# Turning q and k in four quadrants of TensorE beside the score steps, with score steps that run over pair borders

## The chip, the cores and the metric

The kernel runs on one core of one Trainium2 chip. The time is the device time of one launch in microseconds, the median of several runs. A profile of one execution (its trace) shows what each engine did: PE is TensorE's matrix products and PEld its weight loads, DVE is VectorE, ACT ScalarE, POOL GpSimd, SP the engine that mostly issues DMAs.

## What is computed

Attention with a threshold over 8 batches of 8 heads, 576 rows and a head size of 64, all in float32, and then a mixer (a low rank product over the rows and a two-layer channel network) on the result:

```python
scores = scale * np.matmul(q, k.transpose(0, 1, 3, 2))
thresh = np.max(scores, axis=-1, keepdims=True) - tau
scores = np.where(scores >= thresh, scores, -1000000000.0)
attn = np.exp(scores - np.max(scores, axis=-1, keepdims=True))
attn = attn / (np.sum(attn, axis=-1, keepdims=True) + 1e-09)
x = np.matmul(attn, v)                # heads side by side: [8, 576, 512]
h = x.transpose(0, 2, 1) @ U @ V      # rank 32, over the rows
u = x + h.transpose(0, 2, 1)
out = u + np.maximum(u @ w_ch1, 0.0) @ w_ch2      # 512 -> 2048 -> 512
```

## The kernel before

**Tiling.** Two heads of one batch make a pair, 32 pairs in all, worked in couples (two pairs, 64 and 64 columns of the model each). The 576 rows of a head are nine sets of 64 (every ninth row); a full tile is two sets, 128 rows, so a pair has four full tiles and a half one (tile 4), and the half tiles of the two pairs of a couple are put together into one step. A couple is thus nine score steps: tiles 0 to 4 of the first pair and 0 to 3 of the second. There are 144 steps, each with two heads.

**Loads and turning.** `load_tasks` brings q and k of a pair into `qkraw` (rows on the partitions, nine slots of 2 x 64 numbers; slot 4 holds q's tile 4 in the lower partitions and k's in the upper) by eight DMAs, on POOL's queue for all pairs but the first. Scores need the head's 64 numbers on the partitions, so `prepare_tasks` turns them: `turn_main` makes four TensorE transposes of 128x128 for q (L518) and four for k, each four into one PSUM bank, and `copy_main` (L524, ScalarE) copies the bank to `qkT`; `turn_rest` makes one transpose for the two half tiles (L531), `copy_rest` (L537) copies it. `qkT` is a ring of two, `qkraw` too. A pair's loads wait until the turns of the pair two before are done.

**Scores.** `scores` (L587) makes one or two steps in one task. Each product takes 64 partitions (one head) and gives 64 rows, so TensorE runs as four quadrants of 64x64: the row half is the head, the column half the half of the tile. The moving k is cut into two pieces (`PIECES`). PSUM has eight banks of 512 float32 columns; six of them are two `trio` tiles, one for each head, and two steps side by side (slots 0 and 1) fill the columns 224 to 1376 of a trio (`score_cols`). A task of two steps therefore holds all six banks, one of a single step holds banks 0, 1, 3 and 4 (`KEPT`). All other products (transposes included) use the array as 128x128.

**Softmax.** For each step and head, `weigh` (L616, VectorE) scales the scores into a buffer `s_sb` (a ring of seven) and takes their minimum after the sign is turned; `threshold` (L632) and `exponential` (L639) run on ScalarE; `select` (L646, VectorE) compares, multiplies and sums into `w_ring`. POOL copies the last columns twice (L664), a DMA transpose on SP's queue (or TensorE, L677) turns the weights, and `product` (L746 to L754) multiplies them with v. Then come the low rank products (L811, L826), the sums into x, and for each batch `mixer_tasks`: `up` (L930), `rest` (L946) and `down` (L963), whose outputs leave through the ring `o` of three. Where TensorE would be idle at the start, `fill` issues products without use (L421).

**Order.** Nothing is ordered by hand line by line: `Order.run` is a planner that runs when the kernel is built. Each piece of work is a `Task` with an engine, an estimated cost, the tasks it depends on and the banks it takes. The planner walks through time, at each step starts the task that can start first on some engine, with the ready time plus a table of offsets (`OFF`, by kind of task and stage) as its order, and so writes a fixed order for each engine. It gives PSUM banks (`KEPT` for score tasks, any free bank for others), counts a cost for changing TensorE between quadrants and the whole array (`SWITCH`, `PARTS`), and takes mixer products by due times counted in score steps (`DUE`). `BankOrder` declares which accesses of the two trios need an order, bank by bank.

The loop at the end makes nine steps for a couple: up to pair 1 all alone, from then on the first alone and the other eight by twos.

Of the kernel before, what the change touches and what calls it, by code (L numbers as in the profile page):

```python
# [68 lines left out]
P = 128  # L69
# [7 lines left out]
DM = H * D  # L77
# [10 lines left out]
LONE = 2  # L88

# [4 lines left out]
DUE = (461, 86.25, 1468.5, 516.25, 1049.25, 748, 134.75, 1357.5)  # L94
# [33 lines left out]
class Order:  # L128
# [8 lines left out]
    BEFORE = 0.45  # L137
    PATIENCE = (0, 0.2, 0.1, 0.9, 1.35)
# [7 lines left out]
    PARTS = {"S": "quadrants"}  # L146

    HOLD = (61.76, 61.61, 6.12, 44, 94.32, 94.08, 76.76, 0.01, 9.57)
# [4 lines left out]
        "copy_main": (25.53, 63.74, -194.99, 34.77, -69.14, 17.14, -324, 37.67, -35.45),  # L153
        "copy_rest": (6.5, -40.06, -14.53, 24.12, -4.13, -20.91, -46.23, 54.32, -95.65),
        "copy_tt": (-16.03, -64.1, 20.85, -110.66, 55.87, 62.18, -42.53, -53.37, -25.08),
        "copy_u": (89.47, -53.33, 162.09, -74.19, 7.13, 9.51, -102.11, -20.31, -73.82),
        "copy_u4": (-5.3, -56.82, -16.18, -6.54, 49.93, -37.52, 64.79, -22.2, -18.99),
        "copy_w": (75.7, -4.79, -22.58, 20.52, -4.75, 68.84, -1.46, 27.15, 10.06),
        "down": (52.39, 32.35, 33.69, 38.82, 7.25, -27.49, 1.69, 19.34, 131.97),
        "exponential": (61.02, 15.66, 97.71, -26.58, 23.56, 95.43, 116.8, 90.08, 11.21),  # L160
        "finish": (-53.17, -45.71, 51.42, 30.79, -14.22, -26.29, 28.78, 16.33, -75.01),
        "first": (-56.79, 75.89, 0.92, -55.7, 35.86, -3.48, 9.68, 53.63, 1.2),
        "high": (-129.72, -35.78, 31.87, -6.58, 48.08, -20.33, -28.95, -46.46, 84.01),
        "inverse": (46.71, -32.89, 54.08, 22.1, 122.91, 38.13, 143.23, 39.39, -23.27),
        "join": (2.19, 36.38, 69.81, -65.72, -28.72, -7.68, -26.75, 24.75, -3.5),
        "load": (14.89, -38.6, -1.87, -55.09, 439, 169.52, 202.43, 266.17, -64.61),
        "low": (23.82, 3.88, -45.02, 6.6, -28.12, -60.17, -87.19, -43.1, 26.46),
        "low4": (64.5, 130.96, 545.14, -26.82, 13.94, -59.21, 35.95, 265.72, -23.85),
        "low_part": (30.38, 13.98, -26.01, -41.71, 130.31, 109.34, -20.82, -133.07, -1.88),
        "low_rank": (-57.69, 16.1, -2.98, 31.4, -60.74, 41.37, 38.61, 8.08, -35.05),  # L170
        "make": (-18.31, -192.85, -81.78, -52.29, 6.69, -18.25, 12.16, -35.09, 27.21),
        "narrow": (5.95, 39.32, -9.64, -6.72, 1.46, 29.45, -10.31, 45.69, -47.12),
        "narrow_u": (-45.99, -94.08, -136.7, -16.38, -46.01, -113.33, 15.29, 42.82, -0.02),
        "narrow_u4": (2.02, -41.08, 15.16, 12.95, 69.79, 35.67, -44.1, -54.14, 56.42),
        "norm": (60.22, 26.73, 14.75, 16.35, 28.89, -20.28, -16.45, 55.02, 19.4),
        "product": (-38.14, -97.33, -17.17, 18.14, -78.98, 56.88, 40.12, 68.18, -110.66),
        "relu": (44.72, -2.34, -31.3, -83.46, 20.06, -116.77, 10.32, 4.5, -36.91),
        "rest": (64.49, 74.43, 34.29, 18.04, -20.78, -41.41, -55.22, -17.62, 44.45),
        "scores": (-2.16, -56.15, 42.01, -69.96, -15.23, -44.76, 4.79, -16.69, -3.93),
        "select": (-41.99, 29.22, -2.51, 135.03, 570.07, 400.28, 184.53, 231.57, 188.34),  # L180
        "send": (43.87, 17.75, 5.67, -19.7, -14.51, -9.84, 285.3, 70.92, -48.56),
        "send_u": (54.83, -57.33, -16.36, 177.37, 12.48, 121.89, 19.74, 60.45, 25.84),
        "spread": (-216.88, 63.66, -12.54, -9.53, -23.32, -1.29, -122.3, 43.34, 63.38),
        "spread4": (12.62, -19.59, -18, 54.22, -34.85, 61.33, -24.98, -50.63, -66.91),
        "spread_v": (-113.69, -64.83, 6.03, 44.27, 73.51, -47.79, -27.38, 65.24, 2.79),
        "sum_u": (-64.77, 3.32, 13.18, 117.53, -78.44, -9.21, 87.33, 127.21, -64.36),
        "sum_u4": (-96.51, 65.77, 2.32, 38.3, 44.64, 21.12, -125.78, 37.98, 23.47),
        "sums": (195.64, 23.57, 47.14, -31.56, 10.32, -16.1, 35.4, 4.49, -58.98),
        "threshold": (-37.94, -91.24, -43.1, -296.86, 94.89, 36.19, 66.3, 1.07, 12.5),
        "turn4": (-36.19, -43.45, 5.14, 7.01, 54.44, -61.28, 52.57, 29.57, -92.54),  # L190
        "turn_main": (0.34, 20.57, 26.79, -161.06, 126.25, -30.36, -38.23, -14.86, -5.97),
        "turn_pe": (-0.48, -21.65, -184.33, 36.36, -95.83, 51.55, 181.65, 20.16, -43.63),
        "turn_rest": (-5.99, -37.64, -0.75, 52.43, -6.2, -61.13, -8.69, -94.49, -32.06),
        "turn_u": (-85.8, -3, -69.47, -45.79, 74.76, -7.02, 3.37, 12.83, 72.77),
        "turn_w": (45.6, -1.19, -137.3, 47.86, -48.09, 10.25, -28.07, -30.73, 72.41),
        "twin": (32.78, -132.71, -13.72, -15.07, -38.22, -14.87, -64, 49.79, 55.76),
        "up": (13.07, 75.42, -49.49, -57.58, 68.34, -48.43, 10.3, 58.82, 35),
        "values": (-37.57, -25.94, -48.38, 20.3, -54.04, 26.74, 72.56, -4.07, -32.49),
        "weigh": (-145.66, -20.29, -57.18, 79.45, -16.94, 55.31, 45.2, 33.27, 31.94),
        "weights": (-56.28, 79.24, -10.97, 18.21, -35.76, 31.57, -73.46, 67.52, 113.68),  # L200
# [13 lines left out]
    def run(self):  # L214
# [8 lines left out]
        last = [0.0] * self.nbanks  # L223
        kind = None
# [15 lines left out]
        while left:  # L240
# [5 lines left out]
            soonest = min(last[n] for n in pool)  # L246
            for e in range(5):
                cands = []
                for t in ready[e]:
                    s = max(at[e], t.ready)  # L250
                    if t.banks:
                        s = max(s, soonest)
                    if t.trios:
                        s = max([s] + [last[n] - self.BEFORE * (t.steps == 1)
                                       for n in self.KEPT[t.trios]])
                    if e == POOL and t.dma:
                        s = max(s, lanes[t.ndma - 1 - self.LANES])
                    if s < NEVER:
                        cands.append((s, t))
# [6 lines left out]
            assert best, "no task can start"  # L266
            s, t = best
# [14 lines left out]
            if t.trios:  # L282
                t.got = list(self.KEPT[t.trios])
            elif t.banks:
                t.got = [min((n for n in pool if last[n] <= max(s, soonest)),
                             key=lambda n: (n < 6, n % 3 < 2, last[n]))]
            for n in t.got:
                last[n] = NEVER
# [16 lines left out]
            for f in t.frees:  # L305
                f, part = f if isinstance(f, tuple) else (f, slice(0, 8))
                for n in f.got[part]:
                    last[n] = t.end + self.SIGNAL[e] + self.TO_PE
# [13 lines left out]
def kernel(  # L322
# [64 lines left out]
    qkraw_ring = ring("qkraw", 2, [P, 9, 2, D], FP32)  # L387
    qkT_ring = ring("qkT", 2, [P, 2, S], FP32)
    vh_ring = ring("vh", 2, [P, NT, 2, 2, D])
    NS, NE = 7, 4  # L390
# [9 lines left out]
    uT4_ring = ring("uT4", 2, [P, 4, P])  # L400
    ub_ring = ring("ub", 2, [P, 4, P])
    o_ring = ring("o", 3, [P, DM], FP32)
# [7 lines left out]
    PIECES = (((0, HC), (HC, S)), ((0, 224), (224, S)))  # L410
# [24 lines left out]
    class Batch:  # L435
# [3 lines left out]
        def __init__(self, b, before):  # L439
# [5 lines left out]
            self.tt, self.uT, self.uT4 = tt_ring[b % 2], uT_ring[b % 2], uT4_ring[b // 2 % 2]  # L445

    def load_tasks(p, pr):
# [3 lines left out]
        freed = [got("q", p - 2), got("k", p - 2), got("qk4", p - 2)]  # L451
# [21 lines left out]
        for j in range(2):  # L473
            loads["k"].append(one("k", ek, lo, slice(5, 9), slice(0, 4), j, freed))
            loads["k"].append(one("k", e3 if j else ek, hi, slice(4, 9), slice(4, 9), j, freed))
# [9 lines left out]
    class Pair:  # L485


        def __init__(self, b, hp, bt):
# [6 lines left out]
            self.qkraw, self.tT, self.vh = qkraw_ring[p % 2], qkT_ring[p % 2], vh_ring[p % 2]  # L495
# [14 lines left out]
    def prepare_tasks(p):  # L510
# [3 lines left out]
        before = [got("S", p - 2, 3), got("S", p - 2, 4)]  # L514
        for x, (name, t0) in enumerate((("q", 0), ("k", 5))):
            def turn_main(t, t0=t0):
                for i in range(4):
                    nc.tensor.transpose(bank[t.got[0]][:, i * P:(i + 1) * P],  # L518
                                        pr.qkraw[:, t0 + i, :, :], ident)

            task = add(PE, 0.44, turn_main, loads[name] + before, banks=1, kind="qk")

            def copy_main(_, x=x, task=task):
                nc.scalar.copy(out=pr.tT[:, x, 0:512], in_=bank[task.got[0]])  # L524

            done[name, p] = task
            done[name + "T", p] = add(SCA, 0.47, copy_main, [task, got(name + "T", p - 1)],
                                      frees=[task])

        def turn_rest(t):  # L530
# [568 lines left out]
```

## Time and profile before

| | |
|---|---|
| median of 13 runs | 605.24 us (601.44 to 609.05) |
| the profiled execution | 603.74 us |
| its span, first to last instruction | 602.0 us |
| busy DVE: 288 `select` of 0.860, 288 `weigh` of 0.750 us | 239.3 and 203.2 us |
| busy ACT: 288 `exponential` of 0.775 us | 217.8 us |
| the copies of q and k on ACT: 64 of 128x512, 32 of 128x128 | 37.1 and 8.5 us |
| mean granted TensorE clock | 0.996 |

The span is divided among the lines that ended last (the chain of waits); the chain can be followed from 371.7 us on and consists of TensorE's rows for the greater part:

```profile
PE 29%; DVE 4%; ACT 4%; issue 1%; DVEq 0%; ACTq 0%
```

A line of the page's fifth part reads: source line, engine, operation, output from inputs, shapes, count, then busy us and mean ns of one, then idle time of the engine just before these instructions and what ended most of it. TensorE's instructions overlap one another, so the length of one record says less than the distance between starts.

### The profile page before, as it was taken

What the parts mean: (1) busy time and instruction counts of PE and PEld (TensorE: products, weight loads), DVE (VectorE), ACT (ScalarE), POOL (GpSimd) and SP (SyncE); (2) the same over time, 40 slices, a digit from 0 to 9 for tenths busy, and PEclk for the clock granted to TensorE, in tenths of its full rate; (3) what the DMA queues carried; (4) which work ended last, traced back from release to release, by engine and by line L of the source; (5) the groups of instructions that cost most, each with busy time, mean ns of one, the idle gap of its engine ahead of it and who ended that gap; (6) DMA issues with size and microseconds to landing.
All of it is one profiled execution on the core that took longest, in us unless ns stands there. A gap on an engine that the chain in (4) does not pass through costs nothing. (4 is left out here: it accounts for less than half of the span.)

```text
span 602.0 us, 17115 instructions
## 1 busy us (share of the span) xinstructions
PE 584.3 (97%) x6249; PEld 349.6 (58%) x6249; DVE 522.3 (87%) x1399; ACT 458.3 (76%) x959; POOL 370.5 (62%) x596
## 2 busy tenths in 40 slices
PE   7998889999999999999999999999999999999996
PEld 3455665666666566555665656565566666556642
DVE  4889899999999999999988999999999999994101
ACT  5657799998799866897789865897699986784540
POOL 9968576687888864576676665776677633342000
PEclk9999899999999999999999999999999999999999
DMA  7799979987999789989999999887999987667203
GB/s 161 115 176 156 166 129 157 152 150 131 203 179 182 129 182 192 182 146 146 203 152 162 147 178 191 157 161 152 197 164 152 180 153 149 123 96 131 45 1 87
DMA packets 222771, 90.48 MB, mean 150 GB/s; under 512 B 200800, under 2 KB 213040, under 8 KB 222688
## 3 DMA queue, kind: packets, MB, share of 16 engines
q1 hardware_dynamic: 207680, 66.30, 67.2%
q0 software_dynamic: 14048, 22.76, 20.4%
q8 instruction: 49, 0.80, 0.6%
q10 hardware_dynamic: 960, 0.34, 0.2%
q14 instruction: 34, 0.28, 0.2%
HBM read 37.90 MB, written 9.44 MB: 79 GB/s over the span
## 5 line engine op out<-in xcount | busy, mean ns | idle before, releaser
L639 ACT ACTIVATE e_sb<-s_sb,m 128x576 bf16<-128x576 f32 x288 | 217.8, 775 | 42.3 <-DVE s_sb L616 32.6
L646 DVE SCALAR_TENSOR_TENSOR w_ring<-s_sb,thr,e_sb 128x576 bf16<-128x576 f32 x288 | 239.3, 860 | 8.6 <-ACT e_sb L639 3.9
L616 DVE TENSOR_SCALAR_CACHE_REDUCE s_sb<-trio 128x576 f32<-128x576 f32 x288 | 203.2, 750 | 16.1 <-PE trio L587 14.7
L587 PE MATMUL trio<-qkT 64*64 64x288 f32 (+2 forms) x2304 | 163.3, 412 | 0.5 <-DVE x L791 0.3
L664 POOL COPY w_ring<-w_ring 128x128 bf16<-128x128 bf16 (+1 forms) x168 | 71.6, 437 | 106.0 <-DVE w_ring L646 85.7
L587 PEld LDWEIGHTS trio<-qkT 64*64 64x64 f32 x2304 | 83.4, 133 | 57.0 <-issue 11.7
L458 POOL DMA_DIRECT2D qkraw<-in_q_dram x125 | 82.3, 663 | 25.0 <-PE bank L518 21.7
L798 POOL TENSOR_TENSOR x<-x,rec 128x256 f32<-128x256 f32 (+1 forms) x84 | 69.1, 825 | 37.0 <-DVE x L791 28.8
L963 PE MATMUL bank<-W2b,R 128*128 128x512 bf16 x368 | 90.1, 379 | 0.4 <-ACT qkT L524 0.3
L963 PEld LDWEIGHTS <-R 128*128 128x128 bf16 x576 | 53.8, 98 | 54.1 <-issue 1.5
L458 POOL DMA_DIRECT2D qkraw<-in_k_dram x125 | 81.3, 657 | 3.1 <-issue 2.2
L930 PE MATMUL bank<-uT,W1b 128*128 128x512 bf16 x320 | 77.8, 379 | 0.7 <-ACT R L920 0.4
L930 PEld LDWEIGHTS <-W1b 128*128 128x128 bf16 x512 | 47.1, 98 | 53.3 <-issue 5.4
L553 POOL TENSOR_TENSOR vh<-vraw_ring,vh 64x128 bf16<-64x128 f32 x64 | 55.8, 872 | 14.0 <-ACT vh L546 7.6
L750 PEld LDWEIGHTS <-wT_ring 128*128 128x128 bf16 x896 | 56.0, 98 | 7.5 <-issue 2.0
L920 ACT ACTIVATE R<-bank 128x512 bf16<-128x512 f32 x91 | 52.5, 595 | 4.8 <-PE bank L930 3.0
L930 PE MATMUL trio<-uT,W1b 128*128 128x512 bf16 x192 | 48.1, 379 | 0.2 <-DVE s_sb L616 0.2
L963 PE MATMUL trio<-W2b,R 128*128 128x512 bf16 x208 | 47.5, 379 | 0.0
L632 ACT ACTIVATE thr<-m,tau_t 128x2 f32<-128x2 f32 x144 | 42.0, 294 | 3.6 <-DVE s_sb L616 3.3
L750 PE MATMUL bank<-vh,wT_ring 128*128 128x128 bf16 x624 | 44.5, 219 | 0.0
L975 DVE TENSOR_TENSOR o<-bank,x 128x512 f32<-128x512 f32 x23 | 15.8, 688 | 32.1 <-PE bank L963 31.9
L746 PE MATMUL bank<-vh,wT_ring 128*128 128x64 bf16 x176 | 33.9, 193 | 0.0
(105 smaller groups left out, 720.1 us busy)
## 6 DMA issues: line engine op xcount, KB each, us to landing
out_dram<-o SPq DMA_DIRECT2D x71, 128.0 KB, 2.9
vraw_ring<-in_v_dram SPq DMA_DIRECT2D x32, 160.0 KB, 3.9
qkraw<-in_k_dram POOLq DMA_DIRECT2D x63, 80.0 KB, 4.5
qkraw<-in_q_dram POOLq DMA_DIRECT2D x62, 80.0 KB, 4.3
vraw_ring<-in_v_dram SPq DMA_DIRECT2D x32, 128.0 KB, 4.1
qkraw<-in_q_dram POOLq DMA_DIRECT2D x63, 64.0 KB, 3.9
qkraw<-in_k_dram POOLq DMA_DIRECT2D x62, 64.0 KB, 4.3
W1b<-in_moe_w_ch_dram POOLq DMA_DIRECT2D x8, 256.0 KB, 5.4
```

What stands on the lines that cost most here:

```text
L458: queue.dma_start(pr.qkraw[part, to, j, :], src[:, j, of, :])
L553: nc.gpsimd.tensor_tensor(out=pr.vh[part, tiles_, :, h, :], in0=raw[part, tiles_], in1=pr.vh[part, tiles_, :, 0, :], op=ALU.subtract)
L587: mm = nc.tensor.matmul(cols[part, lo:hi], a.tT[hs, 0, rows], a.tT[hs, 1, lo:hi], start=True, stop=True)
L616: nc.vector.tensor_scalar(out=s_sb, in0=score_cols(slot, x), scalar1=-scale, scalar2=None, op0=ALU.mult, op1=ALU.min, accum_out=m[:, x:x + 1])
L639: nc.scalar.activation(out=e_sb, in_=s_sb, func=ACT.Exp, bias=m[:, x:x + 1], scale=-1.0)
L646: nc.vector.scalar_tensor_tensor(out=w_sb[:, 0:S], in0=s_sb, scalar=thr_[:, x:x + 1], in1=e_sb, op0=ALU.is_le, op1=ALU.mult, accum_out=pr. ...
L664: nc.gpsimd.tensor_copy(out=w_sb[:, xs, S:640], in_=w_sb[:, xs, 512:S])
L750: nc.tensor.matmul(av[:, 2 * a + j, :], w, pr.vh[:, kt, j, :, :], start=kt == 0, stop=False)
L798: nc.gpsimd.tensor_tensor(out=x, in0=x, in1=over_sum(part), op=ALU.mult)
L920: nc.scalar.activation(out=R2[:, fts, lo:hi], in_=bank[t.got[0]].rearrange("p (f c) -> p f c", c=hi - lo), func=ACT.Relu)
L930: nc.tensor.matmul(bank[t.got[0]], W1b[:, dt, ft * P:(ft + 1) * P], bt.uT[:, dt, :], start=(dt == 0), stop=(dt == 3))
L963: nc.tensor.matmul(ch, R2[:, ft, lo:lo + P], W2b[:, ft, :], start=(ft == 0), stop=(ft == 15))
```

## The change

- q and k are no longer turned by transposes of 128x128. Each block of 64 rows and 64 numbers is multiplied with a 64x64 corner of the identity, in one of the four quadrants: 18 products for q and 18 for k of a pair. The upper 64 partitions' blocks go to one bank, the lower 64 partitions' to another, so a turn needs two banks. `turn_rest` goes away; `qkraw` has ten slots, so that q and k have a tile 4 of their own.
- Each turn is followed by two copies on ScalarE, 320 and 256 columns, out of the two banks.
- The scores of two steps move to the columns 384 to 1536 of a trio, with pieces of 128, 448, 64 and 512 columns. Columns 0 to 383 of banks 0 and 3 are left free, and the planner puts a turn into them: when a task of two steps is about to start and a turn is ready within 0.2 us, the turn is issued just before it (`forced`). A turn that comes after work in 128x128 mode without such a task is held up by 20 us in the planner's list (`LATER`), but not those of the first three pairs. A bank can now be held by two tasks (`held`, `late`).
- From the couple of pairs 4 and 5 on, steps are taken by twos over the border: the ninth step of a couple is left and goes with the first of the next.
- Rings: `qkT` three in place of two, `s_sb` six in place of seven, `o` two in place of three, one `uT4` in place of two.
- `OFF`, `DUE`, `HOLD` have other numbers; the weigh pass of slot 0 is counted to start 0.75 us ahead of the task's end in place of 0.5.

```diff
-                for i in range(4):
-                    nc.tensor.transpose(bank[t.got[0]][:, i * P:(i + 1) * P],
-                                        pr.qkraw[:, t0 + i, :, :], ident)
-            task = add(PE, 0.44, turn_main, loads[name] + before, banks=1, kind="qk")
+                for i in range(NT):
+                    for h in range(2 if i < 4 else 1):
+                        rows = slice(HB * h, HB * h + HB)
+                        for j in range(2):
+                            nc.tensor.matmul(
+                                bank[t.got[h]][D * j:D * j + D, i * HB:i * HB + HB],
+                                pr.qkraw[rows, t0 + i, j, :], ident[rows, rows],
+                                start=True, stop=True)
+            task = add(PE, 0.28, turn_main, loads[name] + before, banks=2, kind="qk" if p > 2 else "qk0")
...
             def copy_main(_, x=x, task=task):
-                nc.scalar.copy(out=pr.tT[:, x, 0:512], in_=bank[task.got[0]])
+                nc.scalar.copy(
+                    out=pr.tT[:, x, :].rearrange("p (i r) -> p i r", r=HB)[:, 0:9:2, :],
+                    in_=bank[task.got[0]][:, 0:NT * HB].rearrange("p (i r) -> p i r", i=NT))
+            def copy_rest(_, cols=cols, task=task):
+                nc.scalar.copy(out=cols[:, :, 1, :],
+                               in_=bank[task.got[1]][:, 0:4 * HB].rearrange("p (i r) -> p i r", i=4))
...
-        def turn_rest(t):
-            nc.tensor.transpose(bank[t.got[0]][:, 0:P], pr.qkraw[:, 4, :, :], ident)
...
-    PIECES = (((0, HC), (HC, S)), ((0, 224), (224, S)))
+    PIECES = (((0, 128), (128, S)), ((0, 64), (64, S)))
-        return trio[j][:, 224 + slot * S:224 + (slot + 1) * S]
+        return trio[j][:, 384 + slot * S:384 + (slot + 1) * S]
...
+            if forced:
+                t, forced = forced, None
+            elif t.trios:
+                for a in ready[PE]:
+                    if a.banks == 2 and a.ready <= s + self.BESIDE:
+                        s, t, forced = max(s, a.ready, last[0], last[3]), a, t
+                        break
...
     for p in range(0, NP, 2):
         prepare_tasks(p)
+        nine = [(p, i) for i in range(NT)] + [(p + 1, i) for i in range(4)]
+        if left:
+            score_tasks(*left, nine.pop(0))
+            value_tasks(p - 1)
         prepare_tasks(p + 1)
-        while n < 9:
-            two = p >= LONE and n
-            score_tasks(*nine[n:n + (2 if two else 1)])
-            n += 2 if two else 1
+        while len(nine) > (1 if p > LONE else 0):
+            two = p >= LONE and len(nine) < 9 or p > LONE
+            score_tasks(*[nine.pop(0) for _ in range(2 if two else 1)])
+        left = nine
```

## The prediction

> **What bounds the kernel now.** I read the engine rows of the page first, then the stages, then the order of work on TensorE in one stretch, then the rows of single groups and the waits.
>
> ```profile
> PE 584.3 (97%) x6249; PEld 349.6 (58%) x6249; DVE 522.3 (87%) x1399; ACT 458.3 (76%) x959; POOL 370.5 (62%) x596
> ```
>
> TensorE is occupied for 97% of the span, VectorE for 87%. The stages (start and end, length, then busy time and count for PE, PEld, DVE, ACT, POOL) say where each has room:
>
> ```profile
> 30.00:100.00 70.00, 63.02 (x907) 41.10 (x905) 64.21 (x181) 56.63 (x114) 46.84 (x82) 0.98 1.07 159
> 100.00:200.00 100.00, 99.06 (x1142) 63.05 (x1141) 95.88 (x258) 90.20 (x193) 79.35 (x129) 1.00 1.02 160
> 400.00:500.00 100.00, 99.69 (x1103) 60.62 (x1105) 98.27 (x264) 83.72 (x178) 63.85 (x99) 1.00 0.93 162
> 500.00:540.00 40.00, 39.68 (x391) 22.50 (x384) 39.65 (x104) 30.11 (x64) 13.63 (x21) 1.00 0.73 127
> 540.00:602.00 62.00, 57.29 (x391) 30.58 (x389) 14.81 (x31) 22.99 (x45) 5.00 (x9) 0.99 0.34 65
> ```
>
> From 100 on TensorE has almost no hole, and after 540, where VectorE has run out of softmax, TensorE still has 57 us of mixer products. So whatever is taken from or given to TensorE moves the end by as much, so long as VectorE keeps pace; from 400 to 540 VectorE is busy 137.9 of 140 us and has nothing to give. The clock is granted at 1.00 nearly throughout, so it changes no duration here.
>
> The timeline of TensorE (start, length, line, tile mode and shape, count; the distance from one start to the next is the price):
>
> ```profile
> 301.69 0.19 PE L746 MATMUL bank<-vh,wT_ring 128*128 128x64 bf16 x1
> 301.82 2.17 PE L587 MATMUL trio<-qkT 64*64 64x288 f32 x32
> 303.92 0.33 PE L531 MATMUL bank<-ident,qkraw 128*128 128x128 f32 x1
> 304.08 0.60 PE L518 MATMUL bank<-ident,qkraw 128*128 128x128 f32 x4
> 304.52 0.60 PE L518 MATMUL trio<-ident,qkraw 128*128 128x128 f32 x4
> 304.96 0.39 PE L750 MATMUL bank<-vh,wT 128*128 128x128 bf16 x4
> ...
> 307.85 1.20 PE L587 MATMUL trio<-qkT 64*64 64x288 f32 x16
> 308.98 1.90 PE L930 MATMUL bank<-uT,W1b 128*128 128x512 bf16 x8
> ```
>
> A transpose costs 0.44/4 = 0.11 us. A task of two score steps takes 303.92 - 301.82 = 2.10, one of a single step 308.98 - 307.85 = 1.13. The difference, 0.97, is 16 instructions that run four at a time, one in each quadrant: four rounds of 288 columns on average, 0.243 each, 0.84 ns per column.
>
> ```profile
> L639 ACT ACTIVATE e_sb<-s_sb,m 128x576 bf16<-128x576 f32 x288 | 217.8, 775 | 42.3 <-DVE s_sb L616 32.6
> ...
> L587 PE MATMUL trio<-qkT 64*64 64x288 f32 (+2 forms) x2304 | 163.3, 412 | 0.5 <-DVE x L791 0.3
> ...
> L587 PEld LDWEIGHTS trio<-qkT 64*64 64x64 f32 x2304 | 83.4, 133 | 57.0 <-issue 11.7
> ```
>
> ```profile
> L518 PE MATMUL bank<-ident,qkraw 128*128 128x128 f32 x140 | 21.1, 275 | 0.0
> L518 PE MATMUL trio<-ident,qkraw 128*128 128x128 f32 x116 | 18.0, 278 | 1.6 <-DVE s_sb L616 1.3
> ```
>
> The costliest groups (count, busy us and mean ns, then idle time before them) hold the row that decides. A score step has 8 products in the code (two pieces, two heads, two halves), 144 steps make 1152, and the row counts 2304: a float32 product is **two** instructions, each with its weight load. L518 has 140 + 116 = 256 = 8 x 32: a transpose is **one**.
>
> **Turning q and k on TensorE.** Taken away: nine transposes a pair, 9 x 0.109 = 0.98 us. Added: two turns of 18 float32 products of 64 columns. The upper row half gets five products in each of its two quadrants (tiles 0 to 4), the lower half four, so the longer quadrant runs 5 products = 10 passes. A pass is 64 x 0.84 = 0.054; a turn 0.54, a pair 1.08. That is +0.10 a pair, **+3.2 us** over 32 pairs. A pass of this width has no row, so I bound it. Below: one pass per product, 0.27 a turn (first rival). Above: the weight load, 133 ns by its row, shows. L518's loads last 141 and come every 109, so at least 32 of a load overlap the next; 101 x 10 = 1.01 a turn, +33 us. I take 0.054, by L587: the same load, there hidden under its pass.
>
> The Trainium skill, TensorEngine Tiling (Array Packing), section Gotcha 2: Feature Incompatibilities, speaks against the change: column tiling excludes the transpose mode for fp32 input, so that the turns must be ordinary products; the trace has float32 transposes in 128*128 mode alone. Its FP8 and Floating Point Precision, section TensorE Precision Notes, gives true fp32 four passes; the trace shows two instructions, and at four of 0.054 a turn would be an estimated 1.08 and the sum 38 us instead of 3.2. The row decides.
>
> **Fewer score tasks.** Up to pair 3 nothing changes in number (9 single tasks, then 1 + 4). The other 14 couples of pairs have 1 + 4 tasks now, 70; run over the borders they are 126 steps in 63 tasks. Seven fewer. A task costs beyond its passes 0.10 going in (301.82 against the end of L746's slot, 301.72), 0.16 within (2.10 - 8 x 0.243) and 0.05 after (L531 takes 0.16, not 0.11): 0.31, so **-2.2 us**. The pieces change from 288, 288, 224, 352 to 128, 448, 64, 512 columns: the same sum, nothing.
>
> **Turns that find no score task beside them** change the mode twice, 0.31. 58 turns from pair 3 on want one of 63 double tasks. Between none and 58 (18 us) I take one in ten, 6: **+1.9**. The first pairs' turns stand where TensorE runs fillers (L421, 84 of them), at nothing.
>
> **Copies on ScalarE.** 2 x 0.58 (128x512) + 0.27 become 2 x (0.42 + 0.37), from 128x256 at 0.367 and 0.8 ns a column more: +0.15 a pair, 4.8 us, under ScalarE's 144 us of idle time. Uncovered it would be 4.8.
>
> **The new neighbours in banks 0 and 3.** ScalarE's copies and VectorE's first weigh passes (L616) now read the same banks; I count the one as waiting for the other. No such pair exists before, so bounds: nothing, or both copies in VectorE's way, 0.79 x 58 = 46 us. After a turn the copies can start when the score task's first two rounds are through (2 x 0.107 = 0.21) and end at 0.63 and 1.00; the weigh can start after slot 0 and slot 1's first piece, 0.97 + 0.11 = 1.08. So a prompt ScalarE is in time. It is busy some 80% there; behind an exponential of 0.775 with a remainder r the weigh waits r - 0.45, on average 0.07 x 0.8 = 0.056, x 58 = 3.2 us. Only where VectorE has no room (400 to 540, a quarter) does it reach the end: **+0.8**. Behind the weigh on VectorE stand the selects, then the weight transposes on SP's queue; and the next score task waits for all four weighs.
>
> The Trainium skill, PSUM — Partial Sum Buffer, section PSUM bank collisions raise a hardware error, says that two engines on one bank and quadrant at once raise an error, two readers too, so they must be kept apart; no run here shows it yet. Without it this term is 0.
>
> **Rings.** Six score buffers, not seven: a double task fills four, so two older ones may be open, not three, and VectorE must have done more selects first, each of which waits for ScalarE. Between nothing and an exponential a task (0.775 x 63 = 49): selects wait for ScalarE 3.9 us in all today; as much again, a quarter of it felt, **+1.0**. Two output buffers are covered by a row of 16 products (3.45 us) against two issues and a landing of 2.9. Loads: eight a pair on POOL's queue as before, one tile of k moved between them. They wait for two turns of the pair two back instead of three, and the turns may now be held up to 20 us in the list:
>
> ```profile
> L458 POOL DMA_DIRECT2D qkraw<-in_q_dram x125 | 82.3, 663 | 25.0 <-PE bank L518 21.7
> ```
>
> POOL already stands 21.7 us for the turns; behind it wait the copies of the weight rows (L664). Its 38% idle and the third qkT buffer cover that; nothing counted.
>
> **Sum:** 3.2 - 2.2 + 1.9 + 0.8 + 1.0 = +4.7. The profiled span is 602.0, its execution 603.74; 606.7 and 608.4 after. The median, 605.24, is 1.5 above that execution: **610**, own range 604 to 616.
>
> **Rivals.**
> - *One pass a product* (17%). For it: no row shows a float32 product with an identity. Against: all of L587's products double, whatever their width. Turns 0.54 a pair, -14.1, with the other terms -12.6: 592.6.
> - *TensorE's holes close* (15%): the turns take no spare bank any more, so mixer products find one. TensorE idles 9.5 us between 30 and 540, 7.0 of it before 100; half to all of it back gives 605 to 600.5. Against: after 100 only 2.5 us can be had.
> - *VectorE sets the end* (15%), slower: L616 waits for copies that stand behind two ScalarE instructions. VectorE idles 24.7 us from 10 to 540, 0.43 for each of 58 turns; from there each wait counts in full. At 0.7: +15.7, 625.6. For it: 98% and 99% busy in the late stages.
> - *Turns stand alone* (6%): 40 of 58 instead of 6, +10.5, 620.5. *Weight loads show* (4%): 640.
>
> The sum as worked out keeps 43%. About 0.3%, 1.8 us, is what a measurement of this kernel can tell from no change. Of the 43, 4 fall within it and 39 are slower; of the holes' 15, 7 faster, 5 same, 3 slower; the one-pass 17 are faster but for 1; the rest, 25, slower. Faster 0.23, same 0.10, slower 0.67. The range goes from the one-pass case, 591, to the VectorE case, 626; outside lie the weight loads and the edges.
>
> **What would show it.** A turn's row in 64*64 mode with x2304 in all (two passes) or x1152 (one); the start-to-start of 36 instructions near 0.54 or 0.27. L587 still x2304, in 77 runs. Waits of L616 for the copies near 3 us or over 25. TensorE busy in 100 to 540 again above 99%, and its tail after VectorE's last select longer by some 5 us. Wrong it is if turns come in at 0.27, or if most have a 128-mode neighbour on both sides.

## The result and the profile after

The changed kernel takes 614.20 us (median of 11 runs, 610.69 to 620.42) against 605.70 of the kernel before (48 runs): a ratio of 1.0149, 95% interval 1.0122 to 1.0177. It is slower by 1.5%, about twice what was forecast (610). The profiled execution took 612.19 us, its span is 610.4 (before 602.0).

The engine rows of the page after (busy us, share of the span, count):

```profile
PE 591.4 (97%) x8295; PEld 343.5 (56%) x8295; DVE 518.8 (85%) x1399; ACT 465.0 (76%) x991; POOL 357.2 (59%) x596
```

The shares are those of before to within three points. Nothing in them tells a reader that 8 us were lost, or where. The groups of instructions answer the question of the passes, and the copies and waits:

```profile
L546 PE MATMUL trio<-ident,qkraw 64*64 64x64 f32 x1656 | 36.8, 223 | 0.6 <-DVE x L799 0.3 <-ACT wT_ring L711 0.2
L546 PE MATMUL bank<-ident,qkraw 64*64 64x64 f32 x648 | 13.9, 219 | 0.0
L611 PE MATMUL trio<-qkT 64*64 64x128 f32 (+3 forms) x2304 | 162.6, 411 | 0.2 <-DVE s_sb L640 0.2
L640 DVE TENSOR_SCALAR_CACHE_REDUCE s_sb<-trio 128x576 f32<-128x576 f32 x288 | 206.0, 750 | 27.5 <-PE trio L611 16.6 <-ACT qkT L555 5.2 <-ACT qkT L560 0.9
L555 ACT COPY qkT<-trio 128x320 f32<-128x320 f32 x46 | 19.7, 429 | 4.6 <-DVE s_sb L640 3.5 <-PE trio L611 0.8
L560 ACT COPY qkT<-trio 128x256 f32<-128x256 f32 x46 | 17.2, 374 | 7.0 <-PE trio L611 6.4
```

The turns' rows have 1656 + 648 = 2304 instructions for 1152 products: two each. The weigh passes (L640) wait 6.1 us in all for copies of q and k, a wait that did not exist before. In the timeline of TensorE a turn and its score task look like this:

```profile
307.38 1.03 PE L987 MATMUL bank<-W2b,R 128*128 128x512 bf16 x4
308.34 0.74 PE L546 MATMUL trio<-ident,qkraw 64*64 64x64 f32 x34
308.86 0.33 PE L611 MATMUL trio<-qkT 64*64 64x128 f32 x2
308.91 0.23 PE L546 MATMUL trio<-ident,qkraw 64*64 64x64 f32 x2
```

The 34 instructions take 308.86 - 308.34 = 0.52 from start to start, and the score's first two start before the turn's last two. Such a task of turn and two steps takes 2.68 in all, one of two steps alone 2.11: a turn costs 0.57. Summed over the whole trace by the distance between starts, the turns take 40.0 us of TensorE (transposes before: 36.5), the score products 152.7 (before 157.6), fillers 29.2 (114 of them; before 21.6, 84), and TensorE is idle for 10.4 (8.5).

All slots without the fillers come to 562.8 us, before to 563.9: the useful work on TensorE became **smaller** by 1.1, and the fillers and the idle time grew by 7.6 and 1.9. Fillers are issued where the planner expects TensorE to wait. The stages show where the time went. TensorE has more holes than before (99.06) between 100 and 200 us:

```profile
100.00:200.00 100.00, 98.23 (x1516) 60.11 (x1514) 91.98 (x251) 88.84 (x191) 73.94 (x122) 1.00 0.98 153
```

VectorE's rows in three stretches (start and end, length, busy time and count, clock, DMA), first before:

```profile
10.00:160.00 150.00, 139.56 (x383) 0.99 1.00 150
160.00:400.00 240.00, 227.84 (x610) 1.00 0.97 171
400.00:550.00 150.00, 144.35 (x384) 1.00 0.87 151
```

and after:

```profile
10.00:160.00 150.00, 131.21 (x364) 0.99 1.01 152
160.00:400.00 240.00, 228.18 (x613) 1.00 1.02 167
400.00:550.00 150.00, 141.79 (x384) 1.00 0.88 147
```

From 10 to 160 us VectorE did 19 instructions and 8.4 us less. From then on it kept pace in instructions (610 and 613, 384 and 384). The same can be read from the 288 selects in the timeline of VectorE (us from the span's start; this table is used throughout):

| kernel | end of select 81 | from there to select 288 | from there to the end | span |
|---|---|---|---|---|
| before | 158.4 | 387.2 | 56.4 | 602.0 |
| after | 167.8 | 387.2 | 55.4 | 610.4 |
| bf16_all | 169.0 | 383.6 | 55.4 | 608.0 |
| both_less | 166.3 | 380.8 | 56.2 | 603.3 |
| double | 184.6 | 414.2 | 55.5 | 654.3 |
| short_turns | 168.7 | 379.5 | 55.4 | 603.6 |
| short_before | 160.3 | 383.7 | 56.3 | 600.3 |
| other_list | 157.6 | 396.9 | 59.0 | 613.5 |

By select 81 (of tile and head, some nine pairs in) the changed kernel is 9.4 us late, as much as at select 288. Over the 207 selects after it both kernels take 387.2 us. The distance isn't steady, though: it is 3.6 us at select 63, 9.2 at 90, 5.3 at 120, 7.8 at 180 and 11.4 at 270 (3.2 to 12.9 in all after select 81), since the order of the selects among VectorE's other work differs too. And each row is one execution: the seven traces with the changed list and no more work than it has (after, bf16_all, bf16_early, both_less, vec_less, short_copies, short_turns) end select 81 between 166.3 and 172.5. So differences of a few us in this table tell nothing by themselves. The question for the experiments was therefore what the turns' work costs, and what the order costs that the planner wrote for everything else.

### The profile page after: what moved, and what is told of

It reads as the page before. It is cut to its first block, busy times and chain, and to the rows that moved or that the text cites. A ratio compares the mean times of both kernels' runs of the same rounds, so it can differ in the third digit from the quotient of the medians.

```text
span 610.4 us, 21337 instructions
## 1 busy us (share of the span) xinstructions
PE 591.4 (97%) x8295; PEld 343.5 (56%) x8295; DVE 518.8 (85%) x1399; ACT 465.0 (76%) x991; POOL 357.2 (59%) x596
## 5 line engine op out<-in xcount | busy, mean ns | idle before, releaser
L670 DVE SCALAR_TENSOR_TENSOR w_ring<-s_sb,thr,e_sb 128x576 bf16<-128x576 f32 x288 | 235.1, 843 | 6.2 <-ACT e_sb L663 1.8
L640 DVE TENSOR_SCALAR_CACHE_REDUCE s_sb<-trio 128x576 f32<-128x576 f32 x288 | 206.0, 750 | 27.5 <-PE trio L611 16.6
L611 PE MATMUL trio<-qkT 64*64 64x128 f32 (+3 forms) x2304 | 162.6, 411 | 0.2 <-DVE s_sb L640 0.2
L688 POOL COPY w_ring<-w_ring 128x128 bf16<-128x128 bf16 (+1 forms) x168 | 67.6, 408 | 134.7 <-DVE w_ring L670 112.0
L611 PEld LDWEIGHTS trio<-qkT 64*64 64x64 f32 x2304 | 68.3, 134 | 36.3 <-issue 29.8
L822 POOL TENSOR_TENSOR x<-x,rec 128x256 f32<-128x256 f32 (+1 forms) x84 | 60.2, 719 | 46.9 <-DVE x L815 32.5
L577 POOL TENSOR_TENSOR vh<-vraw_ring,vh 64x128 bf16<-64x128 f32 (+1 forms) x64 | 56.0, 876 | 17.3 <-ACT vh L570 6.9
L774 PE MATMUL bank<-vh,wT_ring 128*128 128x128 bf16 x704 | 50.6, 219 | 0.1
L546 PEld LDWEIGHTS trio<-ident,qkraw 64*64 64x64 f32 x1656 | 30.5, 134 | 15.3 <-issue 5.9
L770 PE MATMUL bank<-vh,wT_ring 128*128 128x64 bf16 x200 | 38.5, 193 | 0.0
```

Source lines behind the costliest of these rows:

```text
L577: nc.gpsimd.tensor_tensor(out=pr.vh[part, tiles_, :, h, :], in0=raw[part, tiles_], in1=pr.vh[part, tiles_, :, 0, :], op=ALU.subtract)
L611: mm = nc.tensor.matmul(cols[part, lo:hi], a.tT[hs, 0, rows], a.tT[hs, 1, lo:hi], start=True, stop=True)
L640: nc.vector.tensor_scalar(out=s_sb, in0=score_cols(slot, x), scalar1=-scale, scalar2=None, op0=ALU.mult, op1=ALU.min, accum_out=m[:, x:x + 1])
L670: nc.vector.scalar_tensor_tensor(out=w_sb[:, 0:S], in0=s_sb, scalar=thr_[:, x:x + 1], in1=e_sb, op0=ALU.is_le, op1=ALU.mult, accum_out=pr. ...
L688: nc.gpsimd.tensor_copy(out=w_sb[:, xs, S:640], in_=w_sb[:, xs, 512:S])
L774: nc.tensor.matmul(av[:, 2 * a + j, :], w, pr.vh[:, kt, j, :, :], start=kt == 0, stop=False)
```

## The experiments

Times are medians; the ratio is against the kernel before in the same runs (603.7 to 607.1 there). Two theories stood against each other: that the loss is what TensorE has to do for the turns, and that it is the order, in which VectorE waits for others.

**Less work for TensorE, the same order.** Two bf16 products of the upper 16 bits in place of each float32 product, for all pairs, and for the first eight alone (the lower half of each number is left out):

```diff
+                            for _ in range(2):
                                 nc.tensor.matmul(
-                                    pr.qkraw[rows, t0 + i, j, :], ident[rows, rows],
+                                    pr.qkraw[rows, t0 + i, j, :].bitcast(BF16)[:, 1::2], identb[rows, rows],
```

> The changed kernel with the same order of work on every engine; each turn's float32 product is replaced by two bfloat16 products of the upper 16 bits of q and k (the lower 16 bits are left out of the computation, so the scores are those of shortened q and k). The number of passes stays 10 in the longer quadrant, each should fall from 0.057 to about 0.029 us, a turn from 0.57 to about 0.29 us. Theory A (a turn's cost on TensorE counts in full, early and late): 64 x 0.28 = 18 us less than the changed kernel's 614.2, about 596. Theory B (only where TensorE has no hole, from pair 8 on; the early stage is set by the order itself): 48 x 0.28 = 13.4 us less, about 601. If the turns were hidden: no change.

> As the run with cheap turns, but for the first 8 pairs alone (16 of 64 turns; their lower 16 bits are left out). The order stays the same. Theory A (the early turns are not free, they are part of the 8 us that the changed kernel has lost by 160 us): 16 x 0.28 = 4.5 us less, about 610. Theory B (the early loss sits in the order itself, the turns stand in holes there): under 1 us, about 614.

bf16_all took 611.34 (1.0083, 1.0046 to 1.0121): 14 us less on TensorE (turns 26.0 in place of 40.0) bring 3 to 4, less than either theory expected. bf16_early took 614.93 (1.0148, 1.0088 to 1.0208), as the changed kernel: the first pairs' turns are hidden, as forecast (the interval is as wide as the 4.5 us in question, but select 81 ends at 167.5, too). In the table what bf16_all won, it won after select 81; the early loss stayed.

**More work for TensorE, the same order.** Each turn product is issued twice:

```diff
+                            for twice in range(2):
                                 nc.tensor.matmul(
```

> Every turn's products are issued twice, in the changed kernel's order: 34.5 us more for TensorE (64 turns of 0.54), nothing else. If TensorE sets the end: 646 to 650. If the turns mostly lie where TensorE waits or runs fillers (29 us of fillers and 10 us idle): 618 to 630. The distance from 614 over 34.5 us is the share of a turn's cost that reaches the end.

It took 657.13 (1.0821, 1.0766 to 1.0876). The turns' slots grew by 41 us (some 81 in place of 40.0), the time by 43. What is added counts in full, early too (select 81 comes 16.8 later); of what bf16_all takes away only a quarter comes back.

**Less work for VectorE, and for both.** The selects leave out the last 64 key positions:

```diff
+                c = S if n < NW // 2 else 512
                 nc.vector.scalar_tensor_tensor(
-                    out=w_sb[:, 0:S], in0=s_sb, scalar=thr_[:, x:x + 1], in1=e_sb,
+                    out=w_sb[:, 0:c], in0=s_sb[:, 0:c], scalar=thr_[:, x:x + 1], in1=e_sb[:, 0:c],
```

> From the ninth score tile on the select works on 512 of the 576 columns, in the changed kernel's order (the last 64 key positions of the weights are left as they were, so the output is not the reference's). By the slope of about 1.2 ns a column this takes some 75 ns from each of 280 selects, 21 us of VectorE's work; TensorE's work stays. If TensorE sets the end: 612 to 614. If VectorE sets it: 594 to 598. If the two hold each other back by turns, in the order in which the list put them: 604 to 610, about as little as the 3 us that 14 us less of TensorE's work brought.

> The shortened select of vec_less and the cheap turns of bf16_all together: 21 us less for VectorE and 14 us less for TensorE. If one engine alone sets the end, this is no better than the better one of the two single cuts. If they hold each other back by turns, it is more than their sum: at or below 597.

vec_less took 617.21 (1.0152, 1.0087 to 1.0217): nothing won, though its median select is 65 ns shorter (747 against 812, 1.0 ns for each column left out) and VectorE's busy time 12.9 us (505.9 against 518.8). both_less took 607.56 (1.0023, 0.9987 to 1.006), 6.6 below the changed kernel. That is more than the two single gains together, but by no more than the intervals leave open, and not the 17 that I had set as the mark. So neither cut alone brings its time back. That the two engines hold each other back by turns, in a fixed order, fits this and isn't shown by it.

**Fillers.** Those after 25 us are left out:

```diff
-                    self.filler(n)
+                    if at[PE] < 25.0:
+                        self.filler(n)
```

> The changed kernel with the same order, without the products without use that the planner put in after 25 us (some 78 of 114, about 0.22 us each, 17 us of TensorE's time). The computation is whole. Theory A (TensorE is late in the early stage because fillers and turns together take more than the list counted): 4 to 8 us less, 606 to 610. Theory B (they stand in holes): 614 within 2, or slower if the granted clock falls in the early stage.

It took 618.88 (1.02, 1.014 to 1.0259). The windows of TensorE tell why, of few_fills first (busy and count, then granted clock):

```profile
25.00:60.00 35.00, 25.37 (x468) 0.85 1.20 164
60.00:100.00 40.00, 31.97 (x668) 0.88 0.83 132
```

and of the changed kernel:

```profile
25.00:60.00 35.00, 32.11 (x524) 1.00 1.13 163
60.00:100.00 40.00, 35.99 (x680) 0.96 1.01 147
```

Without these fillers (39 of 114 are left) the clock is granted at 0.85. So the 7.6 us of additional fillers are no cost that could be saved by leaving them out. Whether the fillers would stand in holes at an equal clock this run can't tell.

**Another order, the same work.** In the kernel before, the planner is told 0.43 in place of 0.44 for four transposes:

```diff
-            task = add(PE, 0.44, turn_main, loads[name] + before, banks=1, kind="qk")
+            task = add(PE, 0.43, turn_main, loads[name] + before, banks=1, kind="qk")
```

> The kernel before with one number changed: the planner counts a turn of four transposes at 0.43 instead of 0.44 us. Every instruction is the same, but the orders that the planner writes differ, because the tables were found for 0.44. Theory A (the change's loss is work on TensorE): 605 within 2. Theory B (orders found for other numbers lose several us by themselves): 610 to 615, with the loss in the first 160 us, where TensorE has holes.

It took 616.41 (1.0189, 1.0133 to 1.0245). Nothing but the order differs, and the fillers that the planner adds with it (107 in place of 84); it costs about as much as the whole change did. Here the loss lies after select 81 (396.9 in place of 387.2), so lists lose in different places.

**One part alone, with tables sought anew.** For these the three tables were searched so that the planner's own end comes as early as possible, for as long for the one as for the other. The edits, in the order of the expectations: the loop over the borders alone; the turns (and the changed rings) without it, with `add(PE, 0.57, turn_main, ...)`; both; none; the smaller rings alone; turns in quadrants for the first 8 pairs alone; for the other 24 alone; the changed kernel with two `qkT`, seven `s_sb` and three `o`.

> The kernel before with score steps running over pair borders (70 + 7 score tasks instead of 75 + 9, the transposes kept), and tables of the list sought anew for it. Theory S (the loss lies in what the turns themselves cost): 598 to 606, since seven tasks fewer free 2 to 5 us of TensorE. Theory L (the loss is that of one list against another, any new list of a changed program lies within some 10 us of the old): anywhere from 600 to 616. A rival that puts the loss on the border steps: 610 or more.

> The changed kernel without steps over the borders (score tasks as before), turns in four quadrants entered in the list at their measured 0.57 instead of 0.28, and tables sought anew with the same effort as for border_alone. Theory S: 612 to 620, as slow as the changed kernel or slower, even with the right price and its own list. Theory L: 600 to 612, about the kernel before plus the 5 us that turns cost more than transposes at most.

> The changed kernel, turns entered at their measured 0.57, tables sought anew with the same effort. Nothing that is computed differs from the changed kernel, only the order. Theory S: 611 to 618. Theory L: 600 to 609, most of the loss gone.

> The kernel before with tables sought for as long as the others, starting from its own (the list then promises 1.1 us less than its own list): the control for the search. Both theories: 600 to 610; how far it lies from 606 shows what one list against another is worth when nothing else changes.

> The kernel before with the smaller rings of the changed one (six s_sb, two o, one uT4), transposes and score tasks as before, its list sought anew. If the rings are what costs: 617 to 624, as turns_alone and both_relisted. If the prediction's term for them (+1.0) is right: 607 to 612, as before_relisted (608.8).

> The changed kernel (borders, small rings, three qkT) with turns in quadrants for the first 8 pairs only; the other 24 are transposed in 128x128 mode, four to a bank and the two half tiles in a bank of their own. List sought anew. If the first pairs' turns cost the time, where the trace shows it lost: 618 to 624. If the turns beside the score tasks do: 605 to 612.

> The other way about: the first 8 pairs transposed in 128x128 mode, the other 24 turned in quadrants. List sought anew. If the first pairs' turns cost the time: 607 to 612. If the turns beside the score tasks do: 617 to 624. If both do in parts: both runs near 615.

> The changed kernel with two qkT in place of three, and for it seven s_sb and three o, as before. List sought anew, turns at 0.57. If the smaller rings are what costs: 606 to 613. If not: 617 to 626, like both_relisted (624.2).

| kernel | us | ratio (95%) | select 81 ends |
|---|---|---|---|
| before_relisted | 608.77 | 1.0058 (1.0029 to 1.0088) | 162.6 |
| border_alone | 608.37 | 1.0054 (1.0031 to 1.0078) | 161.7 |
| rings_alone | 607.08 | 1.006 (1.0039 to 1.0081) | 161.5 |
| turns_alone | 623.40 | 1.0288 (1.0208 to 1.0368) | 165.9 |
| both_relisted | 624.22 | 1.0305 (1.0262 to 1.0348) | 176.2 |
| turns_rings | 625.32 | 1.0357 (1.0327 to 1.0387) | 162.9 |
| turns_early | 621.29 | 1.0299 (1.0278 to 1.0319) | 170.6 |
| turns_late | 622.54 | 1.0314 (1.0298 to 1.0329) | 167.8 |

Two parts of the change are cleared: steps over the borders and smaller rings stand beside before_relisted to within 0.1%. The loss comes with the turns. But the two halves of the pairs each lose as much as all pairs together, and both_relisted is 10 us slower than the changed kernel, of which it is but another order (110 fillers, not 114); so these lists are of uneven quality, and the row can't be added up. My theory that a new list with the right price would take most of the loss away fell with turns_alone and both_relisted.

**The turning taken away under each list.** These keep the order exactly. From the fourth pair on the copies take 64 columns (short_copies); the turns also have 4 products in place of 18 (short_turns); and under the list of before one transpose of 128x128 takes the place of four, with a copy of 128 columns (short_before). The scores are then not the reference's.

```diff
-                for i in range(NT):
+                for i in range(NT if p < NQ else 1):
                     for h in range(2 if i < 4 else 1):
```

```diff
-                for i in range(4):
+                for i in range(4 if p < 3 else 1):
                     nc.tensor.transpose(bank[t.got[0]][:, i * P:(i + 1) * P],
```

> The changed kernel and its list; from the fourth pair on each of the four copies of a pair takes 64 columns in place of 320 or 256, so that ScalarE has some 0.23 us less in each of 116 copies, 27 us, and VectorE's weigh passes find the banks free earlier (the scores are then not the reference's). If the copies and the waits of the weigh passes for them cost the time: 605 to 609. If they are hidden, as the prediction has it: 612 to 615.

> As short_copies, and the turns themselves have 4 products in place of 18 from the fourth pair on, the ones whose result is still copied: another 58 x 0.4 = 23 us less for TensorE. What is then left of the loss is not the turns' work but the order of everything else: if the work costs the time, 590 to 600, as much below the kernel before as TensorE has less to do than it (some 18 us); if the order of the list does, 603 to 611.

> The kernel before and its list; from the fourth pair on a turn of q or k has one transpose of 128x128 in place of four, and its copy 128 columns in place of 512 (the scores are then not the reference's): 58 x 0.33 = 19 us less for TensorE, 58 x 0.3 = 17 us less for ScalarE. If TensorE sets the end, as the prediction read the profile: 585 to 589. If the list's chain over several engines does: 596 to 603. The distance to short_turns (605.1), which has as little turning to do, is then what the changed list costs the rest of the work.

short_copies took 616.59 (1.0163, 1.0124 to 1.0202): the copies and the waits for them cost nothing (ScalarE's busy time fell by 18.3 us, 446.7 in place of 465.0). short_turns took 605.13 (0.9988, 0.9959 to 1.0017): the turns' slots fell by 22.8 us (17.2 in place of 40.0), the time by 9 to 10. short_before took 603.07 (0.9961, 0.9929 to 0.9993): the transposes' slots fell by 12 us (19.3 in place of 31.3), the time by 2.4. Of 256 transposes 174 are gone there, 19 us at 0.109 each; the slots fell by less because TensorE often has to wait behind one that is left (up to 0.9 us from its start to the next, against 0.11 where more work is ready). The rows of short_turns (PE, PEld, DVE, ACT, POOL as above),

```profile
10.00:160.00 150.00, 134.97 (x1892) 76.29 (x1891) 129.95 (x363) 116.11 (x254) 112.55 (x197) 1.00 0.95 150
160.00:400.00 240.00, 232.28 (x2755) 128.16 (x2753) 230.98 (x622) 191.35 (x439) 158.37 (x256) 1.00 1.02 169
400.00:550.00 150.00, 146.37 (x1634) 80.70 (x1632) 143.78 (x388) 118.05 (x264) 78.67 (x127) 1.00 0.91 150
```

and the same stretches of the changed kernel,

```profile
10.00:160.00 150.00, 141.61 (x2335) 84.33 (x2327) 131.21 (x364) 121.62 (x255) 111.44 (x197) 0.99 1.01 152
160.00:400.00 240.00, 238.77 (x3524) 141.57 (x3516) 228.18 (x613) 197.41 (x429) 153.88 (x248) 1.00 1.02 167
400.00:550.00 150.00, 148.88 (x2000) 85.45 (x1999) 141.79 (x384) 124.08 (x268) 78.69 (x128) 1.00 0.88 147
```

show that most of the work taken away is idle time now. In all TensorE is busy 22.3 us less (569.1 in place of 591.4), and the span is 6.8 shorter. (Busy times of short_before aren't set beside them: its trace holds 6007 products for 6075 weight loads, so 68 records of products are missing.)

These runs split the loss in two ways. **At the end:** with most of the turning gone the two lists are 0.3% apart, 1.6 us, and their ratios, 0.9988 and 0.9961, lie within each other's intervals. Put back, the turns cost 1.6%, 9.8 us (1.0149 against 0.9988), and the transposes 0.4%, 2.4 us. So of the 9 us that the change costs some 7 come with the exchange of transposes for turns, though their slots differ by only 3.5, and under 2 with the rest of the new list, which is not clear of noise. The two runs don't leave equal turning: 17.2 us of slots in short_turns, 25.3 in short_before with the half tiles; so the share of the list may be larger.

**In order of time:** by select 81 the changed list is late by 9.4 us with its turns and by 8.4 without (168.7 against 160.3), and VectorE's share of short_turns' first row, 129.95, is near the changed kernel's 131.21 (before 139.56). So the early lateness is not the turns' work; it is there in every trace of this list. After select 81 short_turns makes up 4.2 us against short_before (379.5 and 383.7), and the changed kernel, with its turns, makes up nothing (387.2 and 387.2).

## Why the prediction was right or wrong

- **Direction and range** were right (slower; 614.2 lies in 591 to 626, and in the likeliest case's 604 to 616). The size was not: 4.7 forecast, 8.5 measured.
- **Two instructions a product** was right (2304), and 0.54 a turn near 0.57 measured; the slots rose by 3.5, forecast +3.2. The prediction set the two instructions against the four passes for true fp32 (the Trainium skill, FP8 and Floating Point Precision, TensorE Precision Notes). That was a wrong reading of the rows: eight bf16 products of 512 columns take 1.73 us (L930), 0.42 ns a column, and a float32 instruction 0.84, so the two instructions of a product take as long as four bf16 columns, and as a price the four passes agree with the trace. What doesn't follow is four instructions of 0.054, a turn of 1.08.
- **Score tasks** are 77, as forecast. Their slots fell by 4.9, not 2.2, but not as the prediction meant it: at their medians (24 tasks of 1.13 and 60 of 2.10 before, 10 of 1.13 and 67 of 2.11 after) the tasks' own time falls by less than 1 us, and some 4 us come from tasks of before that took longer, a single one up to 2.07. The price of a mode change isn't measured by this. From pair 3 on one turn stood without a score task (at 32.4 us), not six (+1.9 forecast).
- **Copies** take 0.43 and 0.37 (0.42, 0.37 forecast) and are hidden, by short_copies.
- **Neighbours in banks 0 and 3**: 6.1 us of waits, forecast 3.2, of which 0.8 were to be felt; short_copies felt none. **Rings** +1.0: rings_alone shows nothing, and the selects wait 1.8 us for the exponentials, less than the 3.9 before. The two output buffers weren't covered: VectorE waits 6.3 us for outputs to leave (L999, none before), but after 540 us, where the tail is no longer than before.
- **The step that failed** is the first one: "whatever is taken from or given to TensorE moves the end by as much, so long as VectorE keeps pace". What is given does (double: 43 for 41 us). What is taken comes back only in part: 2.4 of 12 us before (short_before), 3 to 4 of 14 (bf16_all) and 9 to 10 of 23 (short_turns) after. I read this from a busy share of 99%, which tells that an engine is never free, not that it is what the others wait for. From it followed a sum in which the transposes were credited in full. They were worth 2.4 us where most of them were taken away, the turns 9.8, and this exchange, not the 3.5 us between their slots, is the greater part of the loss. Why turns come back in time more than transposes the runs don't show.
- **A term at nothing.** The sum had no term for the order, which the planner wrote anew. "The first pairs' turns stand where TensorE runs fillers, at nothing" is right of their work (bf16_early), and silent on the rest: with or without that work VectorE falls 8 to 10 us behind by 160 us. At the end under 2 us of this are left when the turning is taken away, and that is within the noise. From select 81 on, where I placed most of the +4.7, the changed kernel takes as long as the one before (387.2).
- **The rivals.** One pass a product: no. TensorE's holes close: no, fillers and idle time grew. VectorE sets the end by waits for copies: no, vec_less and short_copies. The signs that I named as proof held in part (passes, tasks), which shows that they tested the prices and not the premise; waits of L616 came to 6.1, between the two marks. The last, TensorE above 99% from 100 to 540, failed (98.23 of 100 between 100 and 200), and the tail did not grow by 5 us (55.4 against 56.4), which spoke against TensorE as the only bound at once.

Left open is why the orders found for turned kernels run late before select 81 (162.9 to 176.2, those with transposes 157.6 to 162.6). A rule of the new structure may force it (two banks at once for a turn, its place directly ahead of a score task), or the lists may not be as good. Two runs speak for the lists, without settling it: turns_rings turns all pairs in quadrants and ends select 81 at 162.9, as before_relisted does (162.6), and loses its time later (398.4 to select 288); turns_late transposes the first eight pairs as before and is late all the same (167.8). No version tried that computes the whole result beats the kernel before.

## What to carry to other kernels

Before pricing a change by the work of one engine, ask of the profile whether that engine's work, taken away, would come back as time: a busy share near 100% doesn't say so. Taking the work away under the same order, on both sides of the change, does. Where a planner writes the order, a change to its input is also a new order, and that alone was worth nearly 10 us here (0.43 for 0.44), twice the sum of the change's own terms; so the range needs that term, and a comparison needs the same order on both sides. Compare progress too (the n-th select in both timelines), at several points and in more than one trace: the distance between these two kernels was 3 to 13 us, by the point, after the first quarter.

## What was not expected of the hardware

- The clock that is granted to TensorE fell to 0.85 between 25 and 60 us, and to 0.88 up to 100, when the fillers were left out; with them it stood at 1.00 and 0.96. The Trainium skill (TensorE: Matmul & The Clock Gate, Part 1: The HAM clock gate) has the clock depend on how busy the array has lately been, and this agrees (TensorE was busy 25.4 of 35 us without them, 32.1 with them).
- A turn in quadrants and the score products behind it overlap: the score's first instructions start before the turn's last ones (308.86 against 308.91). Pieces of 128, 448, 64 and 512 columns take as long as 288, 288, 224 and 352 (2.11 against 2.10 a task).
